# Nine loads of the first tile issued at other places of the plan: the second weight piece, and the last rows of the second tile

## The chip, the cores and the metric

The kernel runs on one core of one Trainium2 chip. The metric is the device time of one execution in microseconds (us), as a median over runs. Nothing outside the device counts.

## The reference, cut to what matters

A recurrent attention with a decaying state (4 batches, 8 heads, 768 steps, head size 48) is followed by an MLP with an exact GELU (3072 tokens, 384 to 2048 to 384).

```python
state = zeros((B, H, D, D))
for t in range(S):
    cur = einsum('bhd,bhe->bhde', u[None] * kt, vt)
    y[:, :, t] = einsum('bhd,bhde->bhe', rt, state + cur)
    state = wt[:, :, :, None] * state + einsum('bhd,bhe->bhde', kt, vt)
x = y.transpose(0, 2, 1, 3).reshape(B * S, H * D)
h = x @ w_in
g = 0.5 * h * (1.0 + erf(h / sqrt(2)))
return g @ w_out
```

The attention inputs are float32. The two weight matrices arrive as float64, read as pairs of 32-bit words, and the kernel makes float32 of them on the chip.

## The kernel before

**Tiles and stages.** The 3072 tokens are eight tiles of 384. Stage x of the outer loop interleaves the attention of tile x, the MLP of tile x-1 and the first steps of the attention of tile x+1. Stage 0 has no MLP; it runs the attention of tile 0 in two units, each with half of the heads, and the first steps of tile 1 behind them. There are no loops over time steps: the 64 steps of a chunk are put together in levels of 1, 2, 4, 8, 16 and 32 steps (`LEVELS`). At each level TensorE multiplies keys and queries of every chunk (`products`, L485), the part of the product that belongs to this level is copied into `a_sb` (L581 on VectorE for small levels, L578 on ScalarE for 16), and VectorE multiplies the queries and keys in place with the decay of a block, the update (L563, L552 for the ends). The first level of a unit has two updates of its own (L552), those of the levels 2, 4, 8 and 16 are one instruction each (L563).

After the levels, TensorE turns the keys (`kt_ps`, L754), ScalarE copies them (`g`, L767), TensorE makes the chunk sums (`kv_ps`, L804), VectorE chains the states (L831, ten instructions in a row), and TensorE makes the output of the attention in two parts, inside a chunk (`y_ps`, L857) and from the state before it (L900). VectorE and ScalarE copy it to `xT` (L907, L923); the rows that don't fit go there by small DMAs (L939). `xT` is what the MLP of tile 0 multiplies with `w_in` (`h_ps`, L1299).

**The weights.** `w_in` comes in eight pieces of 768 KB, `w_out` in eight more, counted here from 0 to 15. A piece is loaded as raw words; ScalarE makes three passes over it (`prepare`, L355, L356, L358) and VectorE two (`finish`, L367, L371). Pieces 0, 1 and 2 are loaded as three DMAs of 256 KB each (L230). Each of these is preceded on VectorE by a memset of one column of the place that it will fill (L229), so that the DMA waits until VectorE has come to that point of its own list of work: the memset is how a place in the order of VectorE becomes the time of a load. From piece 3 on a piece is one DMA of 768 KB without a memset (L225).

**The second tile.** The r, k and w rows of tile 1 are loaded in eight shares of 288 KB (`load_second`, `SHARES`), numbered 0 to 7 here, with the same kind of memset before each (L188) and the DMA behind it (L189). The keys of tile 1 end in share 5, its decays lie in shares 5 to 7. They are first read after the attention of tile 0, by L501 (TensorE) and L444 (VectorE).

**What sets the order.** Every engine executes its instructions in the order in which they were written. That order comes from a string for each stage, `PLAN[x]`: each letter takes one step of a generator. In stage 0 "." is a step of unit 0, "s" a step of unit 1, "f" a step of tile 1, "c" a step of the weight conversion, "w" the load of the second tile's v, and "l" the next load with its memset. The loads come in a fixed order:

```python
"l": chain(weight_in(0, True), islice(second, 5), weight_in(1, True), weight_in(2, True), second),
```

So the first three "l" are piece 0, then shares 0 to 4, then piece 1 (three), piece 2 (three), and shares 5 to 7. All of them are issued by SyncE (SP), which issues one DMA after the other and stands still while the one in front waits for its memset. Piece 3 is not an "l": `conversion` issues its load when it has finished piece 0, and the DMA waits for no memset, only for its turn on SP.

Of the kernel before, what the change touches and what calls it, by code (L numbers as in the profile page):

```python
# [36 lines left out]
NC_SP = 8  # L37
HALFWAY = 2
PLAN = {
    0: ".lls.....sslsc.lsslll.sl.sls.f.sl.lfscsl..sfss.lscfs.lscs.s.ssssc..s...ssllls..cs...sw.ccff",  # L40
    1: (
        "..c.cccl.scssxcc.ccs.sc.ssccccsswccc..cl..sccccxcc.ccc.sssclcc..cccwc.wsccscsccc..sscc..l."
        "sclc.w..cccwllwccwlcclcsfccc..cc.fscf..sc..w.s..lf.fwsfl.f..wwfwlfswwfff"
# [1504 lines left out]
```

## Time and profile before

| what | value |
|---|---|
| median of 3 runs | 585.79 us (585.73 to 586.5) |
| the profiled execution: its own time | 584.3 us |
| its span | 582.5 us |
| outside the span | 1.8 us |
| TensorE clock granted | 1.00 |
| VectorE, ScalarE busy | 459.5 us (79%), 299.8 us (51%) |
| DMA, mean over the span | 80 GB/s |
| DMA, mean from 0 to 62 us | 236 GB/s |
| stage 0, up to the first matmul of the MLP (L1299) | 43.78 us |

The page has the engines PE (TensorE matmul), PEld (its weight load), DVE (VectorE), ACT (ScalarE), POOL (GpSimd) and SP (SyncE). A timeline row is: start in us, duration in us, engine, line, operation, tile written <- tiles read, shape, how many in a row, and in brackets how long the engine was idle before it and what it waited for. "issue" there means that the profile shows nothing that it waited for. A row "SPq" is SP's queue issuing DMAs.

### The profile page before, as it was taken

Reading aid. Unit: us, or ns where it says so; the run is one execution under the profiler, and the core shown is the slowest. Engines: PE = TensorE matmul, PEld = TensorE weight load, DVE = VectorE, ACT = ScalarE, POOL = GpSimd, SP = SyncE. Lnnn points to the kernel's source line nnn. Section 1 sums busy time; section 2 is a strip of 40 time slices with the busy share of each in tenths; the row PEclk is TensorE's granted clock in tenths of the full one; section 3 lists DMA queues with packets and bytes.
Section 4 is the critical chain, followed back from the end, with each engine's and each line's share of the span. In section 5 each row is a group of like instructions: output and inputs, shape, how many; then the busy total and the mean of one; then the engine's idle time right before and its main releaser. Section 6 shows DMA issues by size and latency. Waiting matters only on the chain. (4 is left out here: it accounts for less than half of the span.)

```text
span 582.5 us, 17244 instructions
## 1 busy us (share of the span) xinstructions
PE 567.2 (97%) x7407; PEld 505.8 (87%) x7418; DVE 459.5 (79%) x820; ACT 299.8 (51%) x735; POOL 8.0 (1%) x21
## 2 busy tenths in 40 slices
PE   7779999999999999999999999999999999999997
PEld 4566666756799999999999999999999999999997
DVE  7879867999678985798859997598759999884532
ACT  2566999433623656536644456455564366543400
POOL 3100000000000000000000000000000000000000
PEclk9999999999999999999999999999999999999999
DMA  7659661140322202441024201441013200210000
GB/s 243 211 156 337 240 219 56 39 138 3 60 70 66 75 3 36 122 134 57 2 55 122 74 21 21 113 141 37 2 34 115 68 2 1 43 40 7 1 15 34
DMA packets 51003, 46.79 MB, mean 80 GB/s; under 512 B 31728, under 2 KB 36080, under 8 KB 50928
## 3 DMA queue, kind: packets, MB, share of 16 engines
q1 hardware_dynamic: 50832, 45.62, 26.1%
q8 instruction: 58, 0.95, 0.7%
q14 instruction: 17, 0.14, 0.1%
q10 hardware_dynamic: 96, 0.07, 0.1%
HBM read 36.24 MB, written 4.72 MB: 70 GB/s over the span
## 5 line engine op out<-in xcount | busy, mean ns | idle before, releaser
L1087 PE MATMUL h_ps<-xT,w_in_sb 128*128 128x192 f32 x408 | 81.6, 330 | 0.1
L1087 PEld LDWEIGHTS h_ps<-xT,w_in_sb 128*128 128x128 f32 x408 | 67.6, 190 | 3.3 <-ACT g L1119 1.1
L1299 PE MATMUL h_ps<-xT,w_in_sb 128*128 128x384 f32 x192 | 64.2, 490 | 0.1
L1299 PEld LDWEIGHTS h_ps<-xT,w_in_sb 128*128 128x128 f32 x192 | 35.7, 190 | 23.9 <-ACT rkw L1407 0.2
L1313 PE MATMUL o_ps<-w_out_sb,g 128*128 128x192 f32 x224 | 39.5, 326 | 0.0
L1313 PEld LDWEIGHTS o_ps<-w_out_sb,g 128*128 128x128 f32 x224 | 37.0, 190 | 0.3
L669 ACT COPY a_sb<-d 32x256 f32<-32x256 f32 (+8 forms) x90 | 32.6, 363 | 3.3 <-PE d L653 1.4
L1313 PE MATMUL o_ps<-w_out_sb,f 128*128 128x192 f32 x176 | 30.9, 328 | 0.0
L1313 PE MATMUL o_ps<-t,s 128*128 128x192 f32 x176 | 30.8, 328 | 0.0
L1313 PE MATMUL o_ps<-t,g 128*128 128x192 f32 x176 | 30.8, 328 | 0.0
L1313 PE MATMUL o_ps<-w_out_sb,e 128*128 128x192 f32 x176 | 30.7, 328 | 0.0
L1313 PE MATMUL o_ps<-t,e 128*128 128x192 f32 x176 | 30.7, 328 | 0.0
L1087 PE MATMUL u_ps<-s,w_in_sb 128*128 128x192 f32 x160 | 29.5, 327 | 0.0
L1313 PEld LDWEIGHTS o_ps<-t,g 128*128 128x128 f32 x176 | 28.7, 190 | 0.3
L1313 PEld LDWEIGHTS o_ps<-t,s 128*128 128x128 f32 x176 | 28.8, 190 | 0.2
L1313 PEld LDWEIGHTS o_ps<-w_out_sb,e 128*128 128x128 f32 x176 | 28.7, 190 | 0.2
L1313 PEld LDWEIGHTS o_ps<-w_out_sb,f 128*128 128x128 f32 x176 | 28.8, 190 | 0.2
L1313 PEld LDWEIGHTS o_ps<-t,e 128*128 128x128 f32 x176 | 28.7, 190 | 0.2
L1302 ACT ACTIVATE g<-h_ps 128x256 f32<-128x256 f32 (+1 forms) x32 | 13.8, 431 | 28.5 <-PE h_ps L1299 28.4
L485 PEld LDWEIGHTS d<-rkw 64*64 64x64 f32 x1056 | 17.5, 134 | 11.9 <-issue 6.4
L653 PE MATMUL d<-kx,rkw 64*64 64x96 f32 x1056 | 27.1, 247 | 0.0
L401 DVE TRANSPOSE_TENSOR_REDUCE rkw<-kx 128x48 f32<-128x1536 f32 (+3 forms) x24 | 27.0, 1156 | 0.1
(248 smaller groups left out, 1193.4 us busy)
## 6 DMA issues: line engine op xcount, KB each, us to landing
rkw<-in_rkw_dram SPq DMA_DIRECT2D x54, 256.0 KB, 3.6
raw<-in_w_out_dram SPq DMA_DIRECT2D x8, 768.0 KB, 4.9
v_in<-in_v_dram SPq DMA_DIRECT2D x8, 584.0 KB, 4.1
raw<-in_w_in_dram SPq DMA_DIRECT2D x5, 768.0 KB, 8.6
out_dram<-o_sb SPq DMA_DIRECT2D x20, 192.0 KB, 2.0
rkw<-kx SPq DMA_DIRECT2D x72, 48.0 KB, 2.0
rkw<-in_rkw_dram SPq DMA_DIRECT2D x6, 384.0 KB, 5.9
raw<-in_w_in_dram SPq DMA_DIRECT2D x9, 256.0 KB, 4.6
```

The lines of the kernel that those rows point to most:

```text
L401: nc.vector.tensor_reduce(out=fine_sb[:, e, 0:n].rearrange("p a n -> p (a n)"), in_=kx[:, o:o + n * n_m].rearrange("p (m j) -> p m j", j=3 ...
L485: nc.tensor.matmul(d[half[p], g, n * width:(n + 1) * width], lhsT=kc[half[g], b, i, p], rhs=right(half[g], b, i, p), start=True, stop=True)
L653: nc.tensor.matmul(o[half[p], i * 3 * C // 2:(i + 1) * 3 * C // 2], lhsT=kc[half[g], n // NI, n % NI, p], rhs=rx[half[g], 2 * n + p], star ...
L669: nc.scalar.copy(out=at[z, g, first:behind, (a + 1) * h:], in_=d[z, :, :, to] if g == slice(None) else d[z, :, to])
L1087: nc.tensor.matmul(o, lhsT=lhsT, rhs=rhs, start=start, stop=True, skip_group_check=True)
L1299: nc.tensor.matmul(h_ps, lhsT=w_in_sb[:, f // FI, j, f % FI * 128:(f % FI + 1) * 128], rhs=xT[:, j, :], start=(j == 0), stop=(j == NJ - 1))
L1302: nc.scalar.activation(out=gs[group][:, f % FG, 0:t], in_=h_ps[:, 0:t], func=AF.Gelu)
L1313: nc.tensor.matmul(o, lhsT=lhs(j), rhs=rhs(j), start=start and j == 0, stop=(j == HF - 1), skip_group_check=True)
```

## The change

In the string of stage 0 the first three letters "l" that load piece 1 move back: in the order before, they stood one by one behind the update of level 2 in unit 1, behind the update of level 4 in unit 0, and one step (the copy of level 4 in unit 0) later. Now all three stand behind the update of level 4 in unit 1, its third level (1, 2, 4). The last three "l" (shares 5, 6 and 7) move forward: they stood behind the states of unit 0; now they stand behind the update of level 16 in unit 1.

```diff
 PLAN = {
-    0: ".lls.....sslsc.lsslll.sl.sls.f.sl.lfscsl..sfss.lscfs.lscs.s.ssssc..s...ssllls..cs...sw.ccff",
+    0: ".lls.....sslsc.lsslll.sl.ss.f.s.fslllcsl..sfss.lscfs.lscs.llls.ssssc..s...sss..cs...sw.ccff",
```

What that does to the lists of the engines: on VectorE, three memsets of piece 1 and three of the shares stand elsewhere, and nothing else is moved. On SP, shares 5 to 7 now stand ahead of the load of piece 3, which stood ahead of them. The lists of TensorE, ScalarE and GpSimd are the same. The number of instructions and DMAs, and their bytes, are the same.

## The prediction, made before the changed kernel ran

> **What bounds the kernel now.** I read the page first, then the waits of the first 62 us, then timelines of single engines there, the DMA view in windows of 1 to 3 us, and last the busy time in windows of 10 us.
>
> On the page TensorE is busy in 97% of the span, and the chain of waits, followed back from the end, is TensorE's work almost alone; it breaks off before it reaches the part that the diff touches. The other line is a DMA queue that carries instructions.
>
> ```profile
> PE 567.2 (97%) x7407; PEld 505.8 (87%) x7418; DVE 459.5 (79%) x820; ACT 299.8 (51%) x735; POOL 8.0 (1%) x21
> ...
> q8 instruction: 58, 0.95, 0.7%
> ```
>
> 58 packets with 0.95 MB are 16 KB each. TensorE has 7407 + 7418 + 136 semaphore instructions, 14961, and 14961 / 58 is 258 for each packet: this queue brings TensorE's program in blocks of about 256 instructions, or 128 weight loads with their matmuls. The waits of the first 62 us:
>
> ```profile
> ACT f L355 <- DMA raw<-in_w_in_dram: 10.5, 2, 5.8
> ...
> PE d L485 <- issue: 2.5, 3, 1.2
> ...
> PE y_ps L900 <- issue: 1.5, 1, 1.5
> ```
>
> "issue" waits in the middle of a burst of equal matmuls are the thing to see here. TensorE's timeline shows two of them:
>
> ```profile
> 22.40 0.46 PE L485 MATMUL d<-rkw 64*64 64x64 f32 x15
> 24.07 0.73 PE L485 MATMUL d<-rkw 64*64 64x64 f32 x33 [1.21 <-issue]
> ...
> 39.16 0.85 PE L900 MATMUL y_ps<-rkw,st 64*64 64x64 f32 x35 [0.53 <-DVE fence L867]
> 41.54 0.28 PE L900 MATMUL y_ps<-rkw,st 64*64 64x64 f32 x3 [1.53 <-issue]
> ```
>
> The first stop comes after 15 of 48 matmuls, the second after 35 of 38. Counting weight loads, the stops of this stage stand at the 222nd, 349th, 477th and 987th: 127, 128 and 4 x 127.5 apart. They are the block borders. The border between, at the 605th, 733rd and 859th (27.84, 33.40 and 36.18 us), show no stop, or one of 0.26 us at the last. So I call the borders by their times: TensorE stops where the next block is late. The packets of q8 in the trace run from 21.29 to 22.71, 25.43 to 26.36, 29.33 to 31.17, 34.21 to 35.17 and 39.37 to 40.32 us. The stop at 24.07 ends 1.36 us after its packet, those at 36.44 and 41.54 end 1.27 and 1.22 us after theirs. A packet starts after the border before it: 0.8 to 1.5 us later where few loads were in flight (33.40 to 34.21, 27.84 to 29.33), 2.6 and 2.9 us later where many were (18.69 to 21.29; 36.44 to 39.37). The second of these is the stop of 1.53 us, and what was in flight is shares 5 to 7:
>
> ```profile
> 36.41 1.28 SPq L189 DMA_DIRECT2D rkw<-in_rkw_dram  x3
> ```
>
> Two rows of ScalarE show the other chain of this stage:
>
> ```profile
> 25.70 0.93 ACT L355 ACTIVATE f<-raw 128x768 f32<-128x768 f32 x1 [4.71 <-DMA raw<-in_w_in_dram]
> ...
> 32.62 0.86 ACT L767 COPY g<-kt_ps 128x384 f32<-128x384 f32 x2
> ```
>
> From the landing of piece 1 (25.6) to 34.32 ScalarE has no idle time, and the copy L767 that the chunk sums of unit 0 need (TensorE's L804 waits 0.88 us for it) is in that row. VectorE is as full from 34.24 to 39.11. Whatever shifts the end of L900 shifts `xT`, then L1299 at 43.79, and behind that TensorE is full:
>
> ```profile
> 40.00:50.00 10.00, 8.47 (x121) 5.85 (x121) 8.02 (x14) 2.16 (x7) 0.00 (x0) 1.00 0.73 218
> 50.00:60.00 10.00, 10.00 (x171) 6.33 (x170) 9.59 (x13) 9.31 (x17) 0.00 (x0) 1.00 1.02 372
> ```
>
> The columns are the window, its length, the busy time of PE, PEld, DVE, ACT and POOL, the clock, and the DMA share with GB/s. From 50 us on PE is busy throughout, so a shift of the end of stage 0 goes one to one into the total; that is the factor by which I carry it.
>
> **The change part by part.**
>
> *Six memsets on VectorE* are moved, 0.06 us each and begun before the work in front has ended (20.28 and 20.27). Those of piece 1 go to 21.6, ahead of an idle stretch of 1.81 us at 23.03; those of the shares go to 29.2, ahead of one of 0.44. From 36.32 they leave a full stretch. Without that cover the six would cost 0.36 us; I take 0.
>
> *Piece 1.* Its loads were issued at 18.68, 20.37 and 20.86; now the memsets stand behind the update that runs from 20.75 to 21.69, so SP issues at about 21.75, 22.2 and 22.6 (0.1 behind the memset, 0.43 apart, as at 36.41, 36.83 and 37.31). Behind them on SP is only the first load of piece 2, whose memset comes at 22.10: it goes out at 23.1 instead of 22.21, and ScalarE needs piece 2 at 35.36, nine us after its old landing. What ScalarE waits for is the landing of the last part of piece 1. Before, the parts stood in the engines behind share 4, whose last landing is 22.87, and the last part landed at 25.6, on the engine that had brought the instructions; on most others at 23.5 to 24.3. Now the first packets come 0.95 us after the issue (26.81 to 27.75 for a part of piece 2), at 22.7; three parts of 0.7 us each and a receipt of 0.4 give 25.2 at the least. Above, the last issue plus the slowest of the nine parts, 6.9 us, gives 29.5; plus their median, 4.6, it gives 27.2. The nearest row is the part of piece 2 at 26.81, with little ahead of it: 2.8 us, which from 22.6 is 25.4. I take 25.5, no gain and no loss, with -0.4 and +1.6 as ends that I keep, and 3.9 as the worst.
>
> *The stop at 24.07.* Its block was asked for at 18.69 and shares 2 to 4 were in the way, which stay; piece 1 shared the engine at most in the last part, since the packet took 1.43 us where an undisturbed one takes 0.94. Between 0 and 0.5 us of the stop go. On the path it is worth nothing, as ScalarE waits for piece 1 until 25.5 anyway and is full from there. I take 0.
>
> *Shares 5 to 7.* Their memsets come at 29.2, behind the update from 28.24 to 29.20, and SP issues at 29.3, 29.7 and 30.2. Then piece 3 follows at 30.5 instead of 28.52; ScalarE takes it up at 50.34, so 2 us later is hidden. At 36.4 nothing is in flight any more, and the block for 39.74 needs 0.8 to 1.1 us to start, 0.95 to come and 1.25 to be used: 36.44 + 3.2 is 39.65, before it is wanted. The stop of 1.53 us goes: -1.5 (ends: 0 and -1.8, the whole gap between 39.74 and 41.54).
>
> *Piece 3, now in the way of another block.* The block asked for at 33.40 started at 34.21, just when the last packets of piece 3 had left its engine (34.1), and made TensorE wait 0.26 at 36.18. Now 3 x 288 KB stand ahead of piece 3. The three shares took that engine from 37.25 to 39.37, 55 KB in 2.1 us. From the end of the block of 29.33 (about 30.9 now) that is 33.0, and piece 3 with 48 KB another 1.9 at the same rate: 34.9 to 35.0. The block then runs from 35.0 to 35.95 and is used at 37.2 instead of 36.44: the last `kv_ps` of unit 1, and L836 on VectorE that waits for it, are 0.5 late (36.85 to about 37.35), and the next block is ready at 37.2 + 3.2 = 40.4 where it is wanted at 40.25. The three matmuls that ended at 41.82 begin at 40.45 to 40.5 rather than 41.54. So of the 1.5 about 0.5 is given back; ends 0 (the engine serves both queues in turn) and 2.5 (it works piece 3 off as slowly as it did before, 64 KB in the 4.1 us that a block left of 29.05 to 34.1, which ends it at 37).
>
> Sum: 0 + 0 + 0 - 1.5 + 0.5 = -1.0 us. The profiled execution, 584.3 (span 582.5 and 1.8 around it), would be 583.3. The median of the runs is 1.5 above that execution, so the forecast is 585.8 - 1.0 = 584.8.
>
> [...]
>
> **The rivals.**
>
> *Both stops go and none comes* (chance 0.17). The block asked for at 33.40 is served in turn with piece 3, and piece 1 lands at 25.2. For it: the packet of 29.33 did run among loads (1.84 us long). Against it: those of 21.29 and 39.37 waited. Gain 1.5 to 2.2, time 584.0.
>
> *The stop moves to the chunk sums and is longer there* (0.22). Place: border at 36.18, in `kv_ps` of unit 1. For it: in the trace the engine that brings the blocks finished piece 3 1.3 us behind the others, and the start of piece 3 was slow. Deciding point: with the block used at 38.2 or later instead of 36.44 (piece 3 off the engine at 36.0), 38.2 + 3.2 = 41.4 and nothing is won; at the slow rate, 37, TensorE goes on at 39.3, the next border at 42.5, a loss of 1.0, and piece 3 packed as at its old total of 6.1 us behind 2.5 us of shares makes it 2.0. Time 586.2 to 587.8, taken as 587.1.
>
> *Piece 1 lands late* (0.09). ScalarE is full behind it, so each us is a us at L767. At 27.2 it costs 1.6 and takes the 1.5 back: 585.9. At 29.5 it would be 588.2.
>
> **How the numbers follow.** Forecast 0.52, gains of 0.5 to 1.6, so 584.2 to 585.3. 0.2% of 585.8 is 1.17 us, about what a measurement of this kernel can tell from no change: the border is 584.6. Of the forecast 0.28 lies beyond it and 0.24 inside; the first rival, 0.17, beyond; the second 0.20 slower and 0.02 inside; the third 0.05 inside and 0.04 slower. Faster 0.45, same 0.31, slower 0.24. The range goes from 583.9 (most of the first rival) to 587.0 (half of the second).
>
> **What would show it.** Right: ScalarE's L355 on piece 1 at 25 to 26, no "issue" wait above 0.3 us at L900, L1299 at 42.5 to 43, and a q8 packet beginning at 34.5 to 35.5. Wrong: an "issue" wait of over 1 us in L804 or L900 of unit 1, L355 at 27, or L1299 no earlier than 43.8. If L1299 comes earlier and the total doesn't, the factor of one was wrong.

## The result, and the profile after

The changed kernel takes 587.41 us (median of 17 runs, 586.23 to 590.21) beside 585.79 us of the kernel before in the same session (17 runs). The ratio is 1.0038, with an interval of 1.0026 to 1.005: slower by 0.38%, some 2.2 us (the two medians are 1.6 us apart), where 1.0 us less had been forecast. The profiled execution took 587.17 us with a span of 585.3.

Of the two lines of the page that were shown of before, the second is the same, 58 blocks, and in the first TensorE has 1.3 us more of busy time with the same number of instructions.

```profile
PE 568.5 (97%) x7407; PEld 506.9 (87%) x7418; DVE 459.9 (79%) x820; ACT 299.8 (51%) x735; POOL 8.0 (1%) x21
...
q8 instruction: 58, 0.95, 0.7%
```

TensorE's timeline of the first tile, with the columns as before (start, duration, instruction, idle time ahead of it and what ended it):

```profile
23.42 0.73 PE L485 MATMUL d<-rkw 64*64 64x64 f32 x33 [0.66 <-issue]
...
28.14 0.34 PE L485 MATMUL d<-rkw 64*64 64x64 f32 x6 [0.63 <-issue]
...
38.77 0.26 PE L804 MATMUL kv_ps<-v_in,g 64*64 64x48 f32 x3 [1.79 <-issue]
...
40.49 1.59 PE L857 MATMUL y_ps<-a_sb,v_in 64*64 64x64 f32 x43
42.33 1.04 PE L900 MATMUL y_ps<-rkw,st 64*64 64x64 f32 x35 [0.25 <-DVE fence L867]
```

The reader is to see four borders. The stop that was 1.21 us is now 0.66 and ends 0.65 earlier. The border behind it, which had no stop before, has one of 0.63. The border in the chunk sums had 0.26 at 36.44, counted from one weight load to the next (the matmuls there have no idle time), and now has 1.79 of idle time at 38.77. And the last border, with the 1.53 us that the change was to remove, has none: behind the 35 matmuls of L900 the next go on at once. So the stop went where it was expected to go from, and came back one border earlier.

What lies behind the stop in the chunk sums is VectorE, which waits for the last `kv_ps` (its timeline); before, this copy stood at 36.85.

```profile
39.14 0.26 DVE L836 COPY st<-kv_ps 128x96 f32<-128x96 f32 x1 [1.69 <-PE kv_ps L804]
39.44 1.84 DVE L831 SCALAR_TENSOR_TENSOR st<-st,tot_sb,kv_ps 128x48 f32<-128x48 f32 x10
```

ScalarE's timeline gives the other chain:

```profile
26.27 0.95 ACT L355 ACTIVATE f<-raw 128x768 f32<-128x768 f32 x1 [5.81 <-DMA raw<-in_w_in_dram]
...
33.17 0.86 ACT L767 COPY g<-kt_ps 128x384 f32<-128x384 f32 x2
```

Piece 1 is there 0.57 us later than before (25.70), ScalarE is full from there, and the copy for the chunk sums is 0.55 later (32.62).

The busy time in windows (the columns as before, the clock behind POOL) shows a third thing:

```profile
40.00:43.00 3.00, 2.75 (x88) 2.56 (x86) 2.25 (x12) 0.48 (x1) 0.00 (x0) 0.51 0.06 13
43.00:46.00 3.00, 3.00 (x126) 2.75 (x120) 2.75 (x5) 0.95 (x2) 0.00 (x0) 1.00 0.64 171
```

The clock was 0.51 from 40 to 43 us. The whole stretch at half clock runs from 39.5 to 42.9, right behind the stop, and 34 matmuls of L900 and 43 of L857 took 1.55 and 1.59 us in it; in the rows of before, 33 and 44 took 1.17 and 0.90.

The same instruction of both traces, after minus before, puts the parts in order: 0.54 us at the first chunk sums, 2.33 at the border in them, 3.37 just ahead of the last border, 1.58 behind it, 1.62 at 43.5 us and still 1.62 at 188 us. Three small steps follow (0.37 at 189 us, 0.33 at 253, 0.44 at 458), and the end is 2.75 later. So 0.54 is piece 1, 1.79 the stop in the chunk sums, 1.04 mostly the clock, -1.79 the stop that went, and 1.14 the later steps.

The changed kernel was profiled a second time, in an execution of 585.83 us:

```profile
28.38 0.34 PE L485 MATMUL d<-rkw 64*64 64x64 f32 x6 [0.34 <-issue]
...
38.17 0.26 PE L804 MATMUL kv_ps<-v_in,g 64*64 64x48 f32 x3 [0.26 <-issue]
...
41.90 0.28 PE L900 MATMUL y_ps<-rkw,st 64*64 64x64 f32 x3 [0.19 <-issue]
```

There the stop in the chunk sums is 0.26 us, the clock is full, and the loss at L1299 (44.15) is 0.36. What is left there is piece 1, with L355 at 27.17. At the end of the span it is 1.4, as steps of 0.2 to 0.4 at 253, 458 and 505 us follow here too. One profile is not the kernel: the stop at the same border differs by over 1 us between the two executions (1.79 and 0.26). What follows therefore rests on medians, and, where the clock matters, on the mean of those executions that had a clock of 1.000 over the whole span.

### The profile page after: what moved, and what is told of

It is laid out like the page before. It is cut to its first block, busy times and chain, and to the rows that moved or that the text cites. A ratio compares the mean times of both kernels' runs of the same rounds, so it can differ in the third digit from the quotient of the medians.

```text
span 585.3 us, 17246 instructions
## 1 busy us (share of the span) xinstructions
PE 568.5 (97%) x7407; PEld 506.9 (87%) x7418; DVE 459.9 (79%) x820; ACT 299.8 (51%) x735; POOL 8.0 (1%) x21
## 5 line engine op out<-in xcount | busy, mean ns | idle before, releaser
L1299 PE MATMUL h_ps<-xT,w_in_sb 128*128 128x384 f32 x192 | 64.2, 490 | 0.1
L1299 PEld LDWEIGHTS h_ps<-xT,w_in_sb 128*128 128x128 f32 x192 | 35.7, 190 | 23.9 <-ACT rkw L1407 0.2
L1313 PE MATMUL o_ps<-w_out_sb,g 128*128 128x192 f32 x224 | 39.5, 326 | 0.0
```

The source lines that it names most:

```text
L1299: nc.tensor.matmul(h_ps, lhsT=w_in_sb[:, f // FI, j, f % FI * 128:(f % FI + 1) * 128], rhs=xT[:, j, :], start=(j == 0), stop=(j == NJ - 1))
L1313: nc.tensor.matmul(o, lhsT=lhs(j), rhs=rhs(j), start=start and j == 0, stop=(j == HF - 1), skip_group_check=True)
```

## The experiments

Ten more kernels ran and the changed one again, in three sessions on three chips, each beside the kernel before. All edits are on the kernel before. The ratio includes whatever half clock the executions had. The last column is the mean of the executions at full clock, less that of the kernel before in the same session (584.25, 585.11 and 584.64 us), with their number.

| kernel | ratio to before, 95% | at full clock |
|---|---|---|
| shares forward alone | 1.0054 (1.0029 to 1.0079) | +1.8 (2) |
| piece 1 late alone | 1.0057 (1.0037 to 1.0077) | +2.9 (3) |
| both, piece 3 later | 1.0053 (1.0034 to 1.0072) | +2.1 (2) |
| shares forward, piece 3 later | 0.9994 (0.9974 to 1.0014) | -0.2 (9) |
| the changed kernel again | 1.0035 (1.0019 to 1.0051) | +1.9 (6) |
| shares behind piece 3 | 0.9997 (0.9981 to 1.0012) | 0.0 (9) |
| piece 1 together, early | 1.0011 (0.9993 to 1.0029) | +0.5 (5) |
| short warm matmuls | 1.0015 (0.9998 to 1.0031) | none |
| early, shares, piece 3 later | 0.9996 (0.9982 to 1.001) | +0.2 (7) |
| early, shares, piece 3 behind them | 1.0052 (1.0031 to 1.0073) | +2.2 (4) |
| last part of piece 1 alone | 1.0011 (0.9993 to 1.0029) | +0.5 (7) |

**The shares alone.**

```diff
-    0: ".lls.....sslsc.lsslll.sl.sls.f.sl.lfscsl..sfss.lscfs.lscs.s.ssssc..s...ssllls..cs...sw.ccff",
+    0: ".lls.....sslsc.lsslll.sl.sls.f.sl.lfscsl..sfss.lscfs.lscs.llls.ssssc..s...sss..cs...sw.ccff",
```

> Only shares 5 to 7 move forward; piece 1 is loaded where it was. Theory (the block of TensorE's program that is asked for at about 33.4 us waits behind the shares and piece 3): ScalarE's L355 on piece 1 at 25.5 to 25.9 as before, a stop of 1.3 to 2.3 us in L804 of unit 1, no stop over 0.3 us in the last rows of L900, L1299 at 44.2 to 45.0; 0.3 to 1.2 us slower than before. Rival (the bunched piece 1 is what costs): no stop in L804 over 0.5 us and about 1 us faster than before. Rival (the clock): any kernel in which TensorE stands still for about 2 us shows a stretch at half clock behind it and pays 0.8 us or more for that.

Measured: 586.99 us, ratio 1.0054. TensorE's timeline:

```profile
37.86 0.26 PE L804 MATMUL kv_ps<-v_in,g 64*64 64x48 f32 x3 [1.50 <-issue]
43.56 5.76 PE L1299 MATMUL h_ps<-xT,w_in_sb 128*128 128x384 f32 x16
```

The stop has moved as in the changed kernel, with piece 1 where it was (L355 at 25.61). At L1299 this execution is even with before (43.79); it lost 1.65 us much later, where VectorE waited for rows of a later tile. The profile shows the move, and the price only in part: the median needs the pairs below. The loss is larger than the 0.3 to 1.2 us expected; no half clock follows the stop in this profile (its mean clock is 1.000), against the second rival.

**Piece 1 alone.**

```diff
-    0: ".lls.....sslsc.lsslll.sl.sls.f.sl.lfscsl..sfss.lscfs.lscs.s.ssssc..s...ssllls..cs...sw.ccff",
+    0: ".lls.....sslsc.lsslll.sl.ss.f.s.fslllcsl..sfss.lscfs.lscs.s.ssssc..s...ssllls..cs...sw.ccff",
```

> Only the three loads of piece 1 are put together; shares 5 to 7 stay. Theory: L355 on piece 1 at 26.2 to 26.6 (0.55 later, as in the changed kernel), the stop of about 1.5 us in the last rows of L900 stays, no stop over 0.4 us in L804, L1299 at 44.2 to 44.6; 0.5 us slower than before (0.2 to 0.9). Rival (piece 1 is the whole loss): 1.6 to 2.3 us slower.

Measured: 587.66 us, ratio 1.0057, the highest of the eleven (the next two, 1.0054 and 1.0053, lie within its interval). ScalarE's and TensorE's timelines:

```profile
26.97 0.94 ACT L355 ACTIVATE f<-raw 128x768 f32<-128x768 f32 x1 [6.57 <-DMA raw<-in_w_in_dram]
```

```profile
28.86 0.34 PE L485 MATMUL d<-rkw 64*64 64x64 f32 x6 [1.16 <-issue]
...
43.82 0.31 PE L900 MATMUL y_ps<-rkw,st 64*64 64x64 f32 x3 [2.11 <-issue]
...
43.99 3.79 PE L501 MATMUL d<-kx,rkw 64*64 64x96 f32 x94
47.72 0.59 PE L1299 MATMUL h_ps<-xT,w_in_sb 128*128 128x384 f32 x1
```

Piece 1 is 1.27 us late, the border at 28 us has its stop, the old stop at L900 is there and longer, and a stretch at half clock follows it (0.56 from 43.5 to 47 us; the 94 matmuls of L501 took 3.79 us, and 2.17 before). The step that the prediction priced at nothing costs most by itself, more than the expectation and its rival allowed. With the shares forward the old stop at L900 is gone, which may be why the whole change seems to lose less than this half of it (+1.9 against +2.9 at full clock, the latter from three executions; the intervals of the ratios overlap).

**Both, with piece 3 taken out of the way.** Piece 3 is issued together with piece 4.

```diff
+    0: ".lls.....sslsc.lsslll.sl.ss.f.s.fslllcsl..sfss.lscfs.lscs.llls.ssssc..s...sss..cs...sw.ccff",
...
-        for _ in weight_in(i + 3):
+        for _ in chain(*map(weight_in, ((), (3, 4))[i] if i < 2 else (i + 3,))):
```

> The whole change, but piece 3 is loaded together with piece 4, behind the copies of the first tile's output rows, so nothing follows shares 5 to 7 in the queue. Theory (piece 3 behind the shares delays the block): the packet of the instruction queue that follows the border at about 33.9 starts before 35.3, no stop over 0.4 us in L804 or L900, L1299 at 42.6 to 43.4; 0.5 to 1.2 us faster than before. Rival (the shares themselves are enough to delay the block): a stop of 0.8 us or more in L804 stays. Rival (piece 1): no better than half a microsecond slower than before.

Measured: 587.4 us, ratio 1.0053. No border behind 23 us has a stop any more, and the loss stays, so the gain that was expected missed: L355 was at 28.19 in the profile and L1299 at 46.44, with two stretches at half clock, of 3.4 and 6.8 us, on the way (a mean clock of 0.991 over 585.5 us). About 1 us of that was lost by 23 us already, ahead of piece 1. At full clock, too, the kernel is 2.1 us slower than before, so without the stop in the chunk sums the late piece keeps the whole loss.

**The shares, with piece 3 out of the way.**

```diff
+    0: ".lls.....sslsc.lsslll.sl.sls.f.sl.lfscsl..sfss.lscfs.lscs.llls.ssssc..s...sss..cs...sw.ccff",
...
-        for _ in weight_in(i + 3):
+        for _ in chain(*map(weight_in, ((), (3, 4))[i] if i < 2 else (i + 3,))):
```

> Shares 5 to 7 forward, piece 3 together with piece 4, piece 1 loaded where it was. Theory: L355 on piece 1 at 25.5 to 25.9, no stop over 0.4 us in L804 or L900, L1299 at 42.1 to 42.8; 1.0 to 1.8 us faster than before and 0.3 to 0.8 faster than the kernel with both parts and piece 3 later. Rival (the stops take turns whatever is moved): within 0.5 us of before.

Measured: 584.35 us, ratio 0.9994. TensorE's timeline:

```profile
36.42 0.26 PE L804 MATMUL kv_ps<-v_in,g 64*64 64x48 f32 x3 [0.65 <-issue]
...
40.15 0.28 PE L900 MATMUL y_ps<-rkw,st 64*64 64x64 f32 x3 [0.19 <-issue]
```

Both stops are short (the first is above the 0.4 expected), and L1299 begins at 42.40. Against the shares alone this is 2.0 us at full clock: the price of piece 3 behind the shares. Against the kernel above it is 2.3 us: the price of the late piece 1. Both figures lean on two executions at full clock; the ratios are apart as well. But of the 1.3 us by which TensorE is ahead behind L1299, 0.35 is left at the end, and 0.7 of the 1.3 had been there before the shares came into play (L355 at 25.02). The 1.0 to 1.8 us expected were not won: the total is within the rival's 0.5.

**The changed kernel again**, unchanged, for its clock.

> The changed kernel as it is, beside the kernel before in the same set of runs, to have the granted clock of every execution of both. First theory (two terms): executions at full clock 1.8 to 2.6 us over those of before at full clock, because piece 1 lands 0.5 to 1 us later and the stop of 1.5 us comes back at L804; on top of it each stretch of 3.4 us at half clock costs 0.7 to 1.2 us, and more executions have one than before (half of them or more, against about a quarter). Rival (the clock alone): executions at full clock within 0.7 us of those of before.

Measured: 587.36 us, ratio 1.0035. Half of its 12 executions were below full clock, and 54% of the 35 of before; stretches at half clock were 0.60 and 0.54 for each execution. At full clock it is still 1.9 us slower. That the clock alone makes the loss fell, and so did the part of the theory by which more executions than before would have such a stretch.

**The shares behind piece 3.** They stand a little later, behind the step that issues piece 3.

```diff
-    0: ".lls.....sslsc.lsslll.sl.sls.f.sl.lfscsl..sfss.lscfs.lscs.s.ssssc..s...ssllls..cs...sw.ccff",
+    0: ".lls.....sslsc.lsslll.sl.sls.f.sl.lfscsl..sfss.lscfs.lscs.s.ssssclll..s...sss..cs...sw.ccff",
```

> The kernel before with shares 5 to 7 moved forward only to a place behind piece 3, so that piece 3 goes first and the shares follow. Theory (whatever stands in the engines at about 34 us delays the block for the border in L804): a packet of the instruction queue that starts at 35.5 to 37, a stop of 1 to 2.3 us in L804 of unit 1, no stop over 0.3 us in the last rows of L900, 0.2 to 1.5 us slower than before. Rival (only piece 3 behind the shares does it): no stop over 0.5 us in L804 and 1 us or more faster than before.

Measured: 585.34 us, ratio 0.9997. The profile has a stop of 1.49 us in L804 and one of 0.46 in L900: so loads of either kind in front of the block can make the stop. That execution was 0.9 us behind from its first matmuls on (9.69 against 8.82, waiting for its first rows), and had a stop of 1.49 at the border of 24 us, so the size proves little; the median says that this order costs nothing, which neither the theory nor its rival had.

**Piece 1 together, but early**, where its first part was loaded before.

```diff
-    0: ".lls.....sslsc.lsslll.sl.sls.f.sl.lfscsl..sfss.lscfs.lscs.s.ssssc..s...ssllls..cs...sw.ccff",
+    0: ".lls.....sslsc.lsslll.sl.sllls.f.s.fscsl..sfss.lscfs.lscs.s.ssssc..s...ssllls..cs...sw.ccff",
```

> The kernel before with the three loads of piece 1 put together where the first of them was, behind the update of level 2 in unit 1. Theory (the place of the last load is what counts, and the engines are full until 24.5 anyway): L355 on piece 1 at 24.9 to 25.8, no new stop at the border of 28 us, within 0.6 us of before. Rival (loads that stand together are slow or delay the program's blocks wherever they are): L355 at 26.2 or later or a stop of 0.5 us or more at the border of 28 us, 1.5 to 3 us slower than before.

Measured: 585.99 us, ratio 1.0011. L355 begins at 24.24, and the profile is 1.95 us ahead of before at the end of L900. There TensorE waits again:

```profile
42.33 0.88 PE L1299 MATMUL h_ps<-xT,w_in_sb 128*128 128x384 f32 x2 [0.42 <-DMA xT<-ysb]
...
43.84 5.40 PE L1299 MATMUL h_ps<-xT,w_in_sb 128*128 128x384 f32 x16 [0.62 <-DMA xT<-ysb]
```

SP's list suggests the reason: shares 5 to 7, issued from 35.99, stand ahead of the small DMAs to `xT` (38.64), though no run tests this alone. Loading the parts together isn't what costs; where they stand is.

**The last part of piece 1 alone** goes to the new place.

```diff
-    0: ".lls.....sslsc.lsslll.sl.sls.f.sl.lfscsl..sfss.lscfs.lscs.s.ssssc..s...ssllls..cs...sw.ccff",
+    0: ".lls.....sslsc.lsslll.sl.sls.f.sl.fslcsl..sfss.lscfs.lscs.s.ssssc..s...ssllls..cs...sw.ccff",
```

> The kernel before with only the last of the three loads of piece 1 moved, to where the changed kernel has all three. Theory (the landing is late because the engines run dry before the group of three is issued, not because its last load is issued later): with two parts in the engines by then, L355 comes 3.0 to 3.9 us behind the memset of the first part of piece 2, as before (3.6), against 4.3 to 5 with all three moved; within 0.6 us of before. Rival (the place of the last load alone sets the landing): L355 4.2 us or more behind that memset and 1.5 to 3 us slower than before.

Measured: 585.73 us, ratio 1.0011, with L355 at 25.37, where it was before, and 3.26 us behind that memset. One part of 256 KB behind the third update is in time; three of them are not. What this doesn't separate: in the changed kernel SP issues two parts first, so the last one is issued 0.99 us behind the first (22.51), and from the last issue L355 comes after 3.76 us there and 3.64 here. The later issue of the last part explains the difference as well as empty engines do.

**The best of both**: piece 1 early, the shares forward, piece 3 out of the way or not.

```diff
+    0: ".lls.....sslsc.lsslll.sl.sllls.f.s.fscsl..sfss.lscfs.lscs.llls.ssssc..s...sss..cs...sw.ccff",
...
-        for _ in weight_in(i + 3):
+        for _ in chain(*map(weight_in, ((), (3, 4))[i] if i < 2 else (i + 3,))):
```

> Piece 1 as one group at the place of its first part, shares 5 to 7 behind the update of level 16, piece 3 together with piece 4. Theory (three separate terms: landing of piece 1, the border in L804, and the shares in front of the copies of xT): L355 at 24 to 25, no stop over 0.7 us in L804 or L900, no wait of L1299 for the DMAs of xT, L1299 at 40.3 to 41.8; 1.0 to 2.5 us faster than before. Rival (the early piece 1 gives nothing because another wait takes its place): within 0.7 us of before.

Measured: 585.03 us, ratio 0.9996. It is no better than before. In its profile stops of 1.07 and 0.46 us came back in L804 and L900, with nothing behind the shares: the shares alone can make a stop in L804. The same without the second edit, piece 3 issued behind the shares:

> The same, but piece 3 follows shares 5 to 7 in the queue as in the changed kernel. Theory (piece 3 behind the shares delays the block for the border in L804): a stop of 1 to 2.5 us in L804 of unit 1 and a packet of the instruction queue that starts late by as much; 0.7 to 2 us slower than the kernel with piece 3 later, and within 1 us of before. Rival (piece 3 does no harm there): equal to the kernel with piece 3 later within 0.5 us.

Measured: 587.84 us, ratio 1.0052, 2.0 us slower at full clock than its twin. TensorE's timeline has the longest stop of all:

```profile
39.98 0.45 PE L804 MATMUL kv_ps<-v_in,g 64*64 64x48 f32 x4 [3.10 <-issue]
```

The block's packet began at 37.70 here. This pair, with piece 1 early in both, shows the price of piece 3 for the second time.

**Short warm matmuls.** The matmuls on zeros that TensorE makes between the levels, whose result nothing reads, work on 64 columns instead of 512. `z` is 64 for these and stays 512 for the 16 at the start of the kernel.

```diff
-            nc.tensor.matmul(t, lhsT=zeros[:, 0:128], rhs=zeros, start=True, stop=True)
+            nc.tensor.matmul(t[:, 0:z], lhsT=zeros[:, 0:128], rhs=zeros[:, 0:z], start=True, stop=True)
```

> The kernel before with the dummy matmuls between the levels 64 columns wide instead of 512: as many instructions and the same block borders, but TensorE is busy 0.3 us less at each of ten places. They compute nothing that is used. Theory (idle time of TensorE in stage 0 brings stretches of 3.4 us at half clock): more than half of the executions below a mean clock of 0.999 against about a quarter of before, each stretch costing 0.7 to 1.7 us, and the median 0.5 to 3 us slower. Rival (the clock has nothing to do with it): the clocks as before and the median equal or faster by up to 0.5.

Measured: 586.63 us, ratio 1.0015. All 12 executions were below full clock, with 3.0 stretches each, beside 0.54 in those of before: here less work for TensorE between the levels (0.3 us at each of ten places, by the estimate of the expectation) brought more of them. By the medians (1.0 us for 2.5 stretches more) a stretch costs some 0.4 us here, below the expected 0.7; the interval of the ratio (0.9998 to 1.0031) doesn't show the kernel slower.

## Why the prediction was wrong, step by step

**Piece 1 is the step that failed first:** "I take 25.5, no gain and no loss". L355 began at 26.27 and 27.17 in the two profiles. The DMA view of the stretch from 21 to 22.5 us, first of after and then of before, has the reason (packets, bytes and rate in the stretch):

```profile
DMA packets 18, 0.04 MB, mean 29 GB/s; under 512 B 5, under 2 KB 5, under 8 KB 17
```

```profile
DMA packets 247, 0.49 MB, mean 326 GB/s; under 512 B 29, under 2 KB 29, under 8 KB 245
```

Before, the parts stood in the engines behind share 4 and followed it without a gap. Now the engines are nearly empty for 1.5 us before the group's first packets come, at 22.5. The prediction had that start right (22.7), but let the three parts follow in 0.7 us each, with a receipt of 0.4 (in before, the last packet of piece 3 ends at 34.23 and the load has landed at 34.65): their last landings were 24.33, 25.20 and 26.16, so the first took 1.8 us from the first packets, where 1.1 had been put, and the others some 0.9 each. A piece that is waited for had been costed by its last landing in one trace of before, 25.6, which one engine alone had made late (the last of its 16 landings is at 25.59, the one ahead of it at 24.85); the gap in the engines had no term. 25.5 lay at the lucky end of its own bounds (25.2 to 27.2). Counted from the memset of the first part of piece 2, L355 comes after 4.35 to 5.04 us in the four profiles with the three parts late, and after 2.81 to 3.80 in the six that load them one by one.

It has a second price that the prediction did not look for. The block asked for at 23.42 came behind these parts, from 25.69 to 26.57, and makes the stop of 0.63 that ends at 28.14. It cost nothing here, since ScalarE is full from 26.27 on and sets L767. That a block is asked for at the border before it is the author's estimate, from the packets that follow the borders; the trace shows the packets alone.

**The stop at 24.07:** right. 0.55 of it went, worth nothing, since ScalarE waited for piece 1 anyway.

**Shares 5 to 7:** right as to the place. The stop at L900 is gone (at most 0.19), in both profiles of the changed kernel. The size, -1.5, was that of one execution: in two kernels that leave the shares where they were, the last part alone and the short warm matmuls, the same stop is 0.73 and 0.56 in the profile.

**Piece 3 behind the shares is the term that was mis-sized:** the packet of the border in the chunk sums was to begin at 35.0 and be used at 37.2, for 0.5 us. SP's timeline and two stretches of the DMA view (33.3 to 36.5 us, where only q1 has packets, and 36.55 to 37.6):

```profile
29.53 2.10 SPq L189 DMA_DIRECT2D rkw<-in_rkw_dram  x3
31.69 0.42 SPq L225 DMA_DIRECT2D raw<-in_w_in_dram  x1
```

```profile
q1 hardware_dynamic: 561, 1.12, 94.7%
...
q1 hardware_dynamic: 21, 0.03, 7.4%
q8 instruction: 1, 0.02, 5.6%
```

By that estimate the block was asked for at the border at 33.9; the engines worked off the shares and piece 3 at 95% until 36.5, and its packet began at 36.58, when they were nearly done. It was used at 38.77, 1.25 us behind the packet's end as the prediction had it. Of the 1.6 us that the packet was later than forecast, 1.2 is the issue of piece 3 (31.69 instead of 30.5): the three shares took SP 2.10 us instead of 1.2, one of them 1.21 us alone. From that issue to the packet it was 4.9 us, where 4.5 had been worked out. In the other profiles with this order (the changed kernel again, the shares alone, the early piece) it was 4.0, 4.7 and 6.5, so the size of the stop is not a constant: 0.26, 1.50 and 3.10.

The rate behind this term was misread too. The prediction let the three shares leave the block's engine from 37.25 to 39.37, before the packet. The DMA view of before from 38 to 40 us, and the issues from 36 to 38 with the median time to landing, say otherwise:

```profile
q1 hardware_dynamic: 335, 0.70, 96.7%
```

```profile
rkw<-in_rkw_dram SPq DMA_DIRECT2D x3, 288.0 KB, 5.1
```

The loads kept the engines busy until 40 us. Shares 6 and 7 landed in whole at 41.9 and 42.9 (36.83 and 5.1, the median; 37.31 and 5.6, the longest), and no engine had landed its part of share 7 before 40.35: the packet of 39.37 ran among these loads, and 55 KB in 2.1 us is no measured rate.

**The factor of one:** right from 43.5 to 188 us, where the difference stood at 1.62. The steps behind it, 1.1 us in all, come where TensorE waits for VectorE and were not foreseen. The one at 253 us, of 0.3, is in the profile of every kernel with the shares behind the level of 16 steps and in no other; the one at 458 us is in most of those, and in two without. What makes them is open. So a gain wouldn't have come through whole either: with piece 3 out of the way, 1.3 us ahead at 45 us became 0.35 at the end.

**The sum.** Forecast 0 and -1.0; in the profile 0.54 for piece 1, 1.79 - 1.79 for the stop that moved, 1.04 for the clock and 1.14 for the late steps. By the pairs, the shares bring 0.2 us without piece 3 behind them, piece 3 there costs 2.0, and the late piece 1 2.3.

**The rivals.** The second was right about this profile: place, border, and deciding point (38.2; it was 38.77). That its 587.1 is close to the 587.41 measured is partly luck: it has neither the 0.54 of piece 1 nor the clock. Its reason, that the engine that brings the blocks finishes piece 3 last, fits the packet at 36.58; the trace doesn't name the engines.

The third is the other profile up to L1299: piece 1 at 27.2 was to cost 1.6 and take the 1.5 back, and with 27.17 L1299 is 0.36 late. Its 585.9 is a median, though, and by it this execution would have been 584.4; it took 585.83, because of the steps behind. The two were priced as alternatives, 0.22 and 0.09; they hold together, in shares that change from one execution to the next.

The first, that blocks are served in turn with the loads, stays open. At 36.58 and at 37.70 the packet began when the engines were nearly done. At 39.37 in before, which the prediction took as evidence against it, it ran among loads, and so it did at 35.82 in the second profile, where the engines were full from 35 to 36. So these packets neither show turns nor refute them; the trace cannot tell when the block was put in the queue.

**What is not settled.** The prices don't add up: 1.8 and 2.9 us for the halves, 1.9 for both. With piece 3 out of the way the late piece 1 adds 2.3 us (from -0.2 to 2.1), with piece 3 behind the shares it adds 0.1 (from 1.8 to 1.9); piece 3 adds 2.0 with piece 1 in time and nothing with piece 1 late (2.1 without it, 1.9 with it, in two sessions). So either of the two keeps the loss and each hides the other; why they come to the same size isn't shown. Part of it may be that the shares forward remove the stop at L900, which is 2.11 us in the profile of piece 1 alone. How much of the rest is the clock, and how much the few executions at full clock, the runs don't say.

## What to carry to other kernels

Three parts of a load that ScalarE waits for, issued behind one point of the program when the engines had run empty (29 GB/s from 21 to 22.5 us, beside 326 before), were taken up 0.6 to 1.5 us later in the two profiles than the same three spread over the time before: here such a load was better issued while the engines still had others. TensorE's program came in blocks of 16 KB while it ran, and the loads moved out of the way of one block stood in the way of another (the stop of 1.53 us at L900 went, one of 1.79 came in L804), so each border within their reach needs its own sum, from the issue of the last load ahead of it and not of the first. And the stop in L804 was 1.79 and 0.26 us in two executions of one kernel: cost such a stop as a range, and test it by pairs of kernels that differ in one load.

## What the runs showed of the hardware beyond that

TensorE's clock went to half for stretches of 3.4 us (0.50 from 39.5 to 42.9 us in the changed kernel), one of them or two in a row (the 6.8 us of both with piece 3 later), and TensorE was not idle throughout ahead of them: in the 3.4 us ahead of the stretch of the changed kernel it was busy for 1.61, in those of piece 1 alone for 0.93. Over the 17 executions of the changed kernel, with the stretches counted from the mean clock (1.000, 0.997, 0.994 and 0.991), the means were 586.77 us without a stretch, 587.77 with one, 588.27 with two and 589.27 with three: some 0.8 us for each. The runs don't show what sets the length of a stretch, nor how much idle time brings one.

SP took 0.33 to 0.38 us for an issue of shares 5 to 7 in before, and 0.33, 1.21 and 0.38 in the changed kernel. In six profiles with these shares behind the level of 16 steps (the changed kernel twice, the shares alone, the shares with piece 3 later, and the two with piece 1 early) the three took it 1.56 to 2.16 us together, beside 1.28 in before and 1.30 in the kernel that has piece 3 ahead of them. One of shares 0 to 4 took 1.19 us in before and 1.07 in the changed kernel, too, where the other four took 0.33 to 0.38. The traces don't show what such an issue waits for.
